# Attention with a gated feed-forward, one core: new cost entries, an extra VectorE block and new stretch rules in a kernel whose order is recorded by a planner

## The chip, the cores and the metric

The kernel runs on one core of one Trainium2 chip. A core has five engines that run side by side and wait for one another through semaphores: TensorE (PE, matrix products into the PSUM memory), VectorE (DVE), ScalarE (ACT), GpSimd (POOL, which works on the SBUF memory only in this kernel) and SyncE (SP, which issues most of the transfers). The metric is the device time of one execution in microseconds; less is better. The kernel before takes 671.5 us (median of 3 runs, 671.2 to 671.59).

## The reference

One sequence of 2048 positions and width 512. The input is normalised, and goes into an attention with 32 query heads of width 16 that share one key and one value head, and into a feed-forward with 1792 hidden channels. The attention is multiplied by a silu of the feed-forward, and the input is added.

```python
xn = _layernorm(x, axis=-1)                      # 2048 x 512
q = heads(xn @ wq)                               # 32 heads of 16
k = xn @ wk                                      # one head of 16
v = xn @ wv
scores = einsum("bhqd,bkd->bhqk", q, k) * 16 ** -0.5
p = softmax(scores)
s = merge(einsum("bhqk,bkd->bhqd", p, v)) @ wo
h = silu(xn @ w1) @ w2
return x + s * silu(h)
```

## The kernel before, in words

**Tiles and groups.** The queries are cut into 4 chunks of 512, the heads into 8 groups of 4, which gives 32 groups (chunk, heads). Each group meets 16 tiles of 128 keys, so there are 512 pairs of group and tile, and each has 4 blocks, one for each head: a block is the scores of 128 keys against 512 queries. There are 2048 blocks, and each has to be exponentiated. Scores are computed with the keys on the partitions, and a head has only 16 channels, so a score matmul uses 32 of the 128 rows of PE, and four of them, on four row tiles, can run side by side (L571).

**Two ways to exponentiate a block.** *ACT's way*: a run of two blocks is written into one of two PSUM tensors of 1024 columns (psA0 and psA1, in turn), and one activation with Exp turns both into weights in one of eleven slots of `pa_sb` (`exp_A`, L601). *DVE's way*: a block is written into one of three PSUM banks (`D`, `D1`, the two halves of psD, and `F`, psF, which the dense products use too). A tensor_scalar (`exp_D`, L639) adds a constant and clamps, and writes 16-bit integers whose bits, read as bf16, approximate the exponential. When the 4 blocks of a tile are there, POOL makes two more copies, shifted by constants, with int64 adds over four 16-bit numbers at a time (`shift`, L664). A tile of which DVE has only two blocks is shifted by DVE itself (L660). The three copies enter the sum with weights that are built into the values. Slots of DVE's tiles lie in `ph_sb`, and once the input has been used up a fourth lies in `x_sb`.

**PV.** Weights times values are accumulated in psO (`emit_PV`, L723), four column tiles side by side, one for each head of the group; an ACT block needs one such matmul, a DVE block three. When a group is complete, DVE transposes psO (L794), takes reciprocals (L802), multiplies (L811) and, every second group, transposes back (L821).

**Dense work.** Query projections, the two feed-forward products and the output projection go through bank F in jobs of column-tiled matmuls (`emit_job`, L363). Silu is built from a tanh on ACT (`emit_tanh`, L1039; 72 of them) and a multiply on DVE (L1071). `filler` issues matmuls on zeros where the planner finds PE too idle (L363 and, on whole tiles, L370).

**The start.** The first four of 16 row tiles are normalised with ACT's square root. For the three later groups of four tiles, DVE computes statistics (L379, L382), POOL the reciprocal deviation in two operations on 4 columns (`rstd_pow`, L386 an add, L388 a power), and DVE normalises (L400). Transposes, keys and values of these tiles come one after the other between runs of the first groups.

**What sets the order.** The function isn't written in the order in which it runs. `Sched` records operations: `op` appends one to its engine's queue, works out the semaphore waits from what it reads and writes, and estimates with fixed costs when it ends (`model`; 0.4 us on DVE and POOL where no cost is given). The main loop asks these estimates what to record next. Engines then run their queues strictly in the recorded order. In the loop, `score_run` records one ACT run and then calls `fill_D` (L1246), which places DVE blocks into banks that are free, first on the row tiles that the run leaves unused, so that they run beside it. Between two runs the loop fills PE with PV, dense jobs and fillers, up to the time by which ACT needs the next run (`needed`, `target` L1203 to L1213). `v_cand` and `advance_v` choose DVE's next operation.

**Rules per stretch.** A string PLAN names, for each 12 us of the recorder's time on ACT, one row of RULES: 12 numbers such as the slack when a bank counts as free (SLIP), the PE activity under which fillers are issued (KEEP), how long a DVE task waits in favour of blocks (AGE), how far dense work is brought forward (F_BEHIND), or how many tiles DVE may take ahead (LEAD).

Of the kernel before, what the change touches and what calls it, by code (L numbers as in the profile page):

```python
# [13 lines left out]
P = 128  # L14
# [182 lines left out]
def bass_recurrent_scan__grouped_kv_mqa__dense_activation_silu__prompt_kernel(  # L197
# [29 lines left out]
    NWARM = 15  # L227
    NWARM2 = 0
    NWARM3 = 2
    NFRONT = 12  # L230
    AGE2, AGE_ST, FIRST, FRONT_D, FRONT_K, SHORT, ST_EARLY, Q_ACT = 12.0, 1.5, 9.4, 1, 4, 0, 3, 1
    KEEP, ENDQ, ROUND, MAXJOB, AHEAD, Q_EARLY = 0.65, 12, 3.0, 2, 3, 0.18
    LEAD, LEAD_END, SLIP, AGE, AGE1, MARGIN = 3, 1, 0.2, 2.0, 1.2, 0.0
# [1 line left out]
    EV = "vava"  # L235
    PVWAIT, FKEEP = 0.2, 0.75
    NPAIR, LEAD_PAIR = 1, 1


    STRETCH = 12.0  # L240
    PLAN = (
        "AAAOFFAAJFNIAOEJAAGAKAALBACLAMFGKLFPNLFANFAEAAAQHAAODBA"
    )
    RULES = dict(
        A=(0.2, 3.0, 0.65, 10, 1.2, 2.0, 0, 12, 0.2, 3, 3, 0.0),
        B=(0.1, 3.0, 0.65, 10, 1.2, 2.0, 0, 12, 0.2, 3, 3, 0.0),
        C=(0.15, 3.0, 0.65, 10, 1.2, 2.0, 0, 12, 0.2, 3, 3, 0.0),
        D=(0.3, 3.0, 0.65, 10, 1.2, 2.0, 0, 12, 0.2, 3, 3, 0.0),
        E=(0.2, 3.0, 0.65, 11, 1.2, 2.0, 0, 12, 0.2, 3, 3, 0.0),
        F=(0.2, 3.0, 0.65, 10, 1.2, 2.0, 4, 12, 0.2, 3, 3, 0.0),  # L250
        G=(0.2, 3.0, 0.65, 10, 1.2, 2.0, 8, 12, 0.2, 3, 3, 0.0),
        H=(0.2, 3.0, 0.65, 10, 1.2, 2.0, 0, 24, 0.2, 3, 3, 0.0),
        I=(0.2, 3.0, 0.65, 7, 1.2, 2.0, 8, 12, 0.1, 3, 3, 0.0),
        J=(0.25, 3.0, 0.65, 8, 1.2, 2.0, 4, 12, 0.2, 3, 3, 0.0),
        K=(0.2, 3.0, 0.65, 7, 1.2, 2.0, -4, 12, 0.2, 3, 3, 0.04),
        L=(0.2, 3.0, 0.65, 10, 2.0, 3.0, 0, 12, 0.2, 3, 3, 0.04),
        M=(0.1, 3.0, 0.65, 10, 2.0, 3.0, 0, 12, 0.2, 3, 3, 0.0),
        N=(0.2, 3.0, 0.65, 10, 1.2, 1.0, 8, 12, 0.2, 3, 3, 0.04),
        O=(0.15, 3.0, 0.5, 10, 1.2, 2.0, 0, 12, 0.2, 2, 3, 0.0),
        P=(0.3, 3.0, 0.7, 10, 1.2, 2.0, 0, 6, 0.2, 3, 3, 0.0),  # L260
        Q=(0.25, 3.0, 0.65, 9, 1.2, 2.0, 0, 12, 0.2, 4, 3, 0.0),
    )
    NF, F_FROM, F_LEFT, F_LATE, DENSE_END, HOLD, F_BEHIND = 14, 0.05, 9, 3, 0.97, 10, 0

    with ExitStack() as es:
# [109 lines left out]
        def tiles(c):  # L375
            return range(4 * c, 4 * c + 4)
# [7 lines left out]
        def rstd_pow(c):  # L384
            sl = slice(4 * c, 4 * c + 4)
            op("gp", lambda e: e.tensor_scalar(rstd_sb[:, sl], mv_sb[:, sl, 1], LN_EPS, None, op0=ALU.add),  # L386
               reads=[("mv", t) for t in tiles(c)], writes=[("rstd", c)])
            op("gp", lambda e: e.tensor_tensor(rstd_sb[:, sl], rstd_sb[:, sl], mhalf_sb[:, :], ALU.pow),  # L388
               reads=[("rstd", c), "mhalf"], writes=[("rstd", c)])

        def rstd_sqrt(c):
            sl = slice(4 * c, 4 * c + 4)
# [193 lines left out]
        def held(key):  # L586
            return any(p["key"] == key for q in pend for p in q)
# [295 lines left out]
        def behind(by=0):  # L883
            return jst["slots"] + by < all_slots * (progress() - F0) / (F1 - F0)
# [67 lines left out]
        def free_banks(t):  # L952
            return [b for b in BANKS if hold[b] is None and K.ready("pe", [], [b]) <= t]

        def next_job(t):
            if progress() < F0:
                return None
            if sum(h == "job" for h in hold.values()) >= MAXJOB:
                return None
            return next((jb for jb in jobs[:AHEAD] if startable(jb, t)), None)  # L960
# [191 lines left out]
        def needed():  # L1152

            return K.act_end - 0.685 - MARGIN
# [47 lines left out]
        def target(t):  # L1202


            rel, need = max(release(), t), needed()
            if need <= rel:
                return rel
            used = [b for b in dst["fifo"]]
            idle = K.free["v"] + sum(0.6 for b in used)
            frees = [K.ready("pe", [], [b]) for b in BANKS if hold[b] is None]  # L1210
            f = min(frees) if frees else K.free["v"] + 0.65
            x = max(f, idle - 0.43)
            return min(max(rel, x), need) if x <= need + SLIP else need  # L1213

        def score_run(t):
            t = max(t, release())
            if ast["tile"] is None and not left[group_A()]:
                gi = group_A()
                h, kts, rows = halves[gi].pop(0)
                blocks = run_half(gi, h, kts, rows)  # L1220
                fill_D(t, other(rows))
                if tanh_ready(K.act_end - 0.33):
                    emit_tanh()
                exp_A(gi, blocks)
                return
            if ast["tile"] is None:
                gi = group_A()
                tile = ast["tile"] = (gi, left[gi].pop(0))
                if tile in shared:
                    rows = ast["rows"] = shared[tile]  # L1230
                todo = {i for o in dst["open"][:1] for i in o["todo"]}
                if tile not in shared:
                    rows = ast["rows"] = [0, 1] if len(todo & {2, 3}) >= len(todo & {0, 1}) else [2, 3]
                second = tile in shared
            else:
                tile, rows = ast["tile"], other(ast["rows"])
                second = True
            fill_A(tile, rows, state["n"] % 2)
            fill_D(t, other(rows))
            if tanh_ready(K.act_end - 0.33):  # L1240
                emit_tanh()
            exp_A(tile[0], [(i, tile[1], None, 512 * m) for m, i in enumerate(rows)])
            if second:
                ast["tile"] = None

        def fill_D(t, free):  # L1246

            banks = sorted(free_banks(t + SLIP), key=lambda b: (b == "F", K.ready("pe", [], [b])))
            keep = 0
            if "F" in banks and jobs and behind(F_BEHIND) and next_job(t):  # L1250
                keep = 1
            if front:
                keep = max(keep, len(banks) - 1 + sum(h == "blk" for h in hold.values()))
            for bank in banks[:max(0, len(banks) - keep)]:
                pick = [(o, i) for o in dst["open"] for i in o["todo"] if i in free]
                if not pick:
                    pick = [(o, o["todo"][0]) for o in dst["open"] if o["tile"][0] < group_A() or len(left[o["tile"][0]]) < F_LATE]
                if not pick and len(dst["open"]) < 2:
                    new, rows = next_D(t), [0, 1, 2, 3]
                    if new is not None:  # L1260
                        left[new[0]].remove(new[1])
                    else:
                        new, rows = next_half(t), [0, 1]
                    if new is not None:
                        plan_D(new[0], rows)
                        dst["idx"] += 1
                        slot_of[dst["idx"]] = free_slot(new[0])
                        dst["open"].append(dict(tile=new, todo=list(rows), rows=rows, idx=dst["idx"]))
                        pick = [(dst["open"][-1], i) for i in free if i in rows] or [(dst["open"][-1], rows[0])]
                if not pick:  # L1270
                    return
                o, i = pick[0]
                pos = len(o["rows"]) - len(o["todo"])
                o["todo"].remove(i)
                if not o["todo"]:
                    dst["open"].remove(o)
                burst([((o["tile"], i), bank_ap(bank))], [bank])
                dst["fifo"].append(dict(tile=o["tile"], i=i, bank=bank, idx=o["idx"], pos=pos, rows=o["rows"]))
                hold[bank] = "blk"
                if i not in free:  # L1280
                    return
                free.remove(i)
                if not free:
                    return
# [2 lines left out]
        K.free["a"] = max(K.free["a"], FIRST - 0.3)  # L1287
        now, gp_end = 0.0, False
        while state["g"] < NGRP or front or jobs or jst["open"] or tasks:
            (SLIP, ROUND, KEEP, HOLD, AGES["gn1"], AGE, F_BEHIND, ENDQ, PVWAIT, LEAD, AHEAD, MARGIN) = \  # L1290
                RULES[PLAN[min(int(K.act_end / STRETCH), len(PLAN) - 1)]]
            t = max(now, min(K.pe_next("col"), K.pe_next("full")))
            if t > 2000.0:
# [46 lines left out]
            if more and not blocked:  # L1340
                idle = slots - did
                if idle > 0 and K.activity(max(t, K.pe_last + K.pe_len) + 0.216 * idle) < (FKEEP if front else KEEP):
                    filler(idle)
                score_run(t)
                now = 0.0
            elif not did:
                if dst["open"]:
                    fill_D(t, [0, 1, 2, 3])
                now = t + 0.05
            else:  # L1350
                now = 0.0
# [96 lines left out]
```

## Time and profile before

| what | value |
|---|---|
| median of 3 runs | 671.5 us |
| the profiled execution | 673.14 us |
| its span from first to last instruction | 670.3 us |
| mean granted TensorE clock | 0.997 |
| first exponential (L601) starts, last one ends | 10.59 us, 663.14 us |
| tanh (L1039) | 72, mean 781 ns |
| single-block exponentials on DVE (L639, 128x512) | 684, mean 675 to 681 ns by group |
| double-block exponentials on DVE (L639, 128x1024) | 13, mean 1216 to 1224 ns |
| int64 adds on POOL (L664) | 354, mean 1048 ns |
| PV matmuls (L723) on 512 columns from ACT's, DVE's weights | 1330, 2130 |

The span leaves out what lies around the first and the last instruction, so it is compared with spans, and the median with medians. An engine's busy time counts overlapping instructions once. Matmuls are pipelined, so PE's 97% doesn't mean that PE has no room: four column matmuls start within 0.02 us of one another, and the next four 0.216 us later. In a group's line, the figures behind the bar are busy time, the mean duration of one, and the idle time of the engine just before, with what ended most of it.

### The profile page before, as it was taken

The numbers are of one execution on the slowest core, as the hardware profiler recorded it, in microseconds if no ns is written. First come the engines' busy times: TensorE is split into PE (matmuls) and PEld (weight loads), VectorE is DVE, ScalarE is ACT, GpSimd is POOL, SyncE is SP. The second block draws the span as 40 slices with busy tenths as digits, with TensorE's granted clock in tenths as the row PEclk, the third lists the DMA queues.
The fourth block names the chain that finished last, engine by engine and source line by source line (L and its number), as shares of the span: only waits on it lengthen the run. The fifth ranks groups of instructions, "written<-read, shape, count | busy, mean of one in ns | idle before, by whom it ended". The sixth has DMA issues, their size and how long they took to land.

```text
span 670.3 us, 18577 instructions
## 1 busy us (share of the span) xinstructions
PE 649.2 (97%) x8137; PEld 182.2 (27%) x8143; DVE 599.9 (90%) x1008; ACT 657.9 (98%) x755; POOL 375.0 (56%) x379
## 2 busy tenths in 40 slices
PE   8999999999999999999999999999999999999997
PEld 4422222222222222222222222222222222222222
DVE  7899889898888988999899889898899889888997
ACT  6999999999999999999999999999999999999997
POOL 3156546465565655555665566564565547656652
PEclk9999999899999999999999999999999999999999
DMA  6340000000000001000000000010000000000110
GB/s 174 139 147 1 2 2 1 2 1 2 2 1 2 1 18 34 17 2 2 1 2 2 1 2 2 1 34 17 18 2 1 2 2 1 2 2 1 34 33 31
DMA packets 12336, 12.48 MB, mean 19 GB/s; under 512 B 2528, under 2 KB 11744, under 8 KB 12256
## 3 DMA queue, kind: packets, MB, share of 16 engines
q1 hardware_dynamic: 11680, 10.78, 5.2%
q8 instruction: 63, 1.03, 0.6%
q10 hardware_dynamic: 576, 0.52, 0.2%
q14 instruction: 17, 0.14, 0.1%
HBM read 8.95 MB, written 2.10 MB: 16 GB/s over the span
## 4 chain that ended last, share of the span: by engine, by line
ACT 77%; PE 16%; DVE 6%; POOL 1%; DMA 0%; issue 0%; ACTq 0%
ACT pa_sb L601 72%; PE psA L571 5%; PE psO L723 5%; ACT t_sb L1039 5%; PE psF L363 4%; DVE ph_sb L639 1%; DVE stats_sb L379 1%; DVE xn_sb L400 1%; POOL rstd_sb L388 0%; PE psD L571 0%; DVE x_sb L639 0%; DMA x_sb<-in_A_x_dram 0%; PE psD L411 0%; DVE onb_sb L811 0%; PE psD L442 0%
## 5 line engine op out<-in xcount | busy, mean ns | idle before, releaser
L601 ACT ACTIVATE pa_sb<-psA 128x1024 bf16<-128x1024 f32 x669 | 636.5, 1202 | 3.2 <-PE psA L571 1.7
L664 POOL INT64_ADD ph_sb<-ph_sb x292 | 302.3, 1048 | 214.6 <-DVE ph_sb L639 214.4
L639 DVE TENSOR_SCALAR ph_sb<-psD 128x512 int16<-128x512 f32 x513 | 349.5, 692 | 40.1 <-PE psD L571 32.7
L723 PE MATMUL psO<-ph_sb,vaug_sb 128*32 128x512 bf16 x1758 | 218.3, 385 | 0.3
L723 PE MATMUL psO<-pa_sb,vaug_sb 128*32 128x512 bf16 (+1 forms) x1346 | 202.8, 383 | 0.6 <-DVE onb_sb L835 0.6
L571 PE MATMUL psA<-qT_sb,kTa_sb 32*128 32x512 bf16 x680 | 131.9, 384 | 4.5 <-ACT pa_sb L601 3.1
L571 PE MATMUL psA<-qT_sb,kTb_sb 32*128 32x512 bf16 x650 | 126.5, 386 | 7.0 <-ACT pa_sb L601 6.3
L571 PE MATMUL psD<-qT_sb,kTb_sb 32*128 32x512 bf16 x325 | 119.5, 385 | 1.0 <-DVE ph_sb L639 1.0
L571 PE MATMUL psD<-qT_sb,kTa_sb 32*128 32x512 bf16 x311 | 114.0, 384 | 0.0
L664 POOL INT64_ADD x_sb<-x_sb x62 | 64.3, 1049 | 44.9 <-DVE x_sb L639 44.9
L639 DVE TENSOR_SCALAR x_sb<-psD 128x512 int16<-128x512 f32 (+1 forms) x110 | 75.5, 691 | 11.7 <-PE psD L571 10.9
L571 PEld LDWEIGHTS psA<-qT_sb,kTa_sb 32*128 32x128 bf16 x680 | 32.0, 91 | 145.1 <-ACT pa_sb L601 131.2
L571 PEld LDWEIGHTS psA<-qT_sb,kTb_sb 32*128 32x128 bf16 x650 | 30.6, 91 | 144.7 <-ACT pa_sb L601 132.3
L363 PE MATMUL psF<-xnT_sb,w_sb 128*32 128x512 bf16 x896 | 69.6, 386 | 0.0
L363 PE MATMUL psF<-w_sb,u_sb 128*32 128x512 bf16 x896 | 69.2, 384 | 0.0
L723 PEld LDWEIGHTS psO<-ph_sb,vaug_sb 128*32 128x32 bf16 x1758 | 53.9, 95 | 51.2 <-issue 35.3
L723 PE MATMUL psO<-x_sb,vaug_sb 128*32 128x512 bf16 x372 | 65.9, 383 | 0.0
L723 PEld LDWEIGHTS psO<-pa_sb,vaug_sb 128*32 128x32 bf16 x1346 | 49.3, 95 | 43.5 <-issue 34.8
L1039 ACT ACTIVATE t_sb<-psF 128x512 bf16<-128x512 f32 x72 | 56.2, 781 | 0.0
L1071 DVE SCALAR_TENSOR_TENSOR u_sb<-t_sb,psF 128x512 bf16<-128x512 bf16 x56 | 38.2, 682 | 4.8 <-ACT t_sb L1039 3.6
L639 DVE TENSOR_SCALAR ph_sb<-psF 128x512 int16<-128x512 f32 x62 | 42.1, 680 | 0.0
L571 PEld LDWEIGHTS psD<-qT_sb,kTb_sb 32*128 32x128 bf16 x325 | 28.2, 91 | 2.4 <-DVE ph_sb L639 1.4
(125 smaller groups left out, 361.7 us busy)
## 6 DMA issues: line engine op xcount, KB each, us to landing
w_sb<-in_B_w_dram SPq DMA_DIRECT2D x2, 1792.0 KB, 8.9
x_sb<-in_A_x_dram SPq DMA_DIRECT2D x18, 128.0 KB, 2.3
out_dram<-ob_sb SPq DMA_DIRECT2D x14, 128.0 KB, 1.7
x_sb<-in_A_x_dram SPq DMA_DIRECT2D x3, 512.0 KB, 6.5
wop_sb<-in_A_wo_dram SPq DMA_DIRECT2D x1, 512.0 KB, 4.2
wq_sb<-in_A_wq_dram SPq DMA_DIRECT2D x1, 384.0 KB, 6.2
x_sb<-in_A_x_dram ACTq DMA_DIRECT2D x2, 128.0 KB, 2.8
kTb_sb<-kTa_sb SPq DMA_DIRECT2D x16, 16.0 KB, 1.8
```

What stands on the lines that cost most here:

```text
L363: r = e.matmul(bank[32 * i:32 * i + 32, :], lhsT=lhsT[:, 32 * i:32 * i + 32], rhs=rhs, start=start, stop=stop, tile_position=(0, 32 * i), ...
L379: op("v", lambda e: e.bn_stats(stats_sb[:, t, :], x_sb[:, t, :]), reads=[("x", t)], writes=[("st", t)], cost=0.687)
L400: op(eng, lambda e: e.tensor_scalar(xn_sb[:, t % 8, :], x_sb[:, t, :], mv_sb[:, t, 0:1], rstd_sb[:, t:t + 1], op0=ALU.subtract, op1=ALU.mult),
L571: return e.matmul(ap, lhsT=kT_sb[g % 2][32 * i:32 * i + 32, kt * P:(kt + 1) * P], rhs=qT_sb[32 * i:32 * i + 32, c % 2, g // 2, :], start=T ...
L601: d = op("a", lambda e: e.activation(pa_sb[:, sl, :], psA[k][:, :], ACT.Exp, scale=ESCALE), reads=["A%d" % k], writes=[("pa", sl)], cost=2 ...
L639: d = op("v", lambda e: e.tensor_scalar(ph_ap(0, sl, 512 * pos, 512 * pos + m), src, float(PH_ONE + PH_BIAS), 0.0, op0=ALU.add, op1=ALU.ma ...
L664: d = op("gp", lambda e, j=j: e.int64_add(ph_ap(j, sl, 0, 4 * NQ).bitcast(I64), ph_ap(0, sl, 0, 4 * NQ).bitcast(I64), PH_SHIFT[j] * 0x0001 ...
L723: r = e.matmul(psO[32 * i:32 * i + 32, cs], lhsT=vaug_sb[:, p["v"], p["kt"], :], rhs=p["ap"], start=s0, stop=s1, tile_position=(0, 32 * i) ...
L1039: op("a", lambda e: e.activation(t_sb[:, n % 2, :], bank_ap(b), ACT.Tanh, scale=0.5 if jb[0] == "h" else 0.25), reads=[b], writes=[("t", n ...
L1071: op("v", lambda e: e.scalar_tensor_tensor(out=dst, in0=t_sb[:, n % 2, :], scalar=1.0, in1=src, op0=ALU.add, op1=ALU.mult), reads=tk["read ...
```

## The change

The costs of the two POOL operations for the reciprocal deviation are given to the recorder (0.3 and 1.07 in place of the default 0.4 each). A new function `extra_fill`, called behind a run in stretches whose rule has XGAIN under 2, may place one more DVE block: it estimates when DVE will have nothing left, and takes the free bank that is ready soonest, at most XWAIT = 0.3 us from now, if DVE gains more than XGAIN plus the wait. The bank is passed to `fill_D`, which then leaves out its own choice of banks and the reservation of F. The lead of 0.43 in `target` becomes a number of the rule (AIM). NFRONT, the number of tiles before dense jobs may start, goes from 12 to 16. PLAN and RULES get new values, with two more columns (XGAIN and AIM); 14 of the 56 stretches of the new PLAN have an XGAIN under 2.

```diff
-    NFRONT = 12
+    NFRONT = 16
...
+    XHOLD, XTASK, XWAIT, XGAIN, XCOST, XOPEN, XBEH, AIM = 7, 0, 0.3, 9, 1.0, 0, 99, 0.43
...
     PLAN = (
-        "AAAOFFAAJFNIAOEJAAGAKAALBACLAMFGKLFPNLFANFAEAAAQHAAODBA"
+        "AAAJFHIPQRACARAAREKMLBPAHAOQDMDJAAJKHQGGQOFIRNIQFGGEMBBA"
     )
     RULES = dict(
-        A=(0.2, 3.0, 0.65, 10, 1.2, 2.0, 0, 12, 0.2, 3, 3, 0.0),
...
+        A=(0.2, 3.0, 0.65, 10, 1.2, 2.0, 0, 12, 0.2, 3, 3, 0.0, 9, 0.43),
...
+        R=(0.2, 3.0, 0.5, 10, 1.2, 1.5, 0, 12, 0.2, 3, 3, 0.0, 0.35, 0.43),
     )
...
             op("gp", lambda e: e.tensor_scalar(rstd_sb[:, sl], mv_sb[:, sl, 1], LN_EPS, None, op0=ALU.add),
-               reads=[("mv", t) for t in tiles(c)], writes=[("rstd", c)])
+               reads=[("mv", t) for t in tiles(c)], writes=[("rstd", c)], cost=0.3)
             op("gp", lambda e: e.tensor_tensor(rstd_sb[:, sl], rstd_sb[:, sl], mhalf_sb[:, :], ALU.pow),
-               reads=[("rstd", c), "mhalf"], writes=[("rstd", c)])
+               reads=[("rstd", c), "mhalf"], writes=[("rstd", c)], cost=1.07)
...
-            x = max(f, idle - 0.43)
+            x = max(f, idle - AIM)
...
-        def fill_D(t, free):
+        def extra_fill():
+
+            t = K.pe_last + K.pe_len
+            if sum(held(("pa", k)) for k in range(NPA)) >= XHOLD or group_A() >= NGRP or (XOPEN and jst["open"]) or (XBEH < 99 and behind(XBEH)):
+                return
+            advance_v(t + 0.05)
+            vfree = K.free["v"] + 0.62 * len(dst["fifo"]) + sum(tk["cost"] for tk in tasks if XTASK and all(n in tok for n in tk["need"]) and K.ready("v", tk["reads"], tk["writes"]) < t + 0.6)
+            ride = max(needed(), t + 0.2) + 0.43
+            best = None
+            for b in BANKS:
+                if hold[b] is None and (b != "F" or not jobs or not behind(F_BEHIND) or not next_job(t)):
+                    r = max(t, K.ready("pe", [], [b]))
+                    gain = max(vfree, ride) - max(vfree, r + 0.43)
+                    if r <= t + XWAIT and gain > XGAIN + XCOST * (r - t):
+                        if best is None or r < best[0]:
+                            best = (r, b)
+            if best is None:
+                return
+            fill_D(best[0], [0, 1, 2, 3], [best[1]])
+
+        def fill_D(t, free, only=None):
 
             banks = sorted(free_banks(t + SLIP), key=lambda b: (b == "F", K.ready("pe", [], [b])))
+            if only:
+                banks = only
             keep = 0
-            if "F" in banks and jobs and behind(F_BEHIND) and next_job(t):
+            if not only and "F" in banks and jobs and behind(F_BEHIND) and next_job(t):
                 keep = 1
...
                 score_run(t)
+                if XGAIN < 2:
+                    extra_fill()
```

More of the change, by code (lines that the diff above doesn't have):

```diff
@@ L237, in bass_recurrent_scan__grouped_kv_mqa__dense_activation_silu__prompt_kernel @@
     NPAIR, LEAD_PAIR = 1, 1
+    XHOLD, XTASK, XWAIT, XGAIN, XCOST, XOPEN, XBEH, AIM = 7, 0, 0.3, 9, 1.0, 0, 99, 0.43
     STRETCH = 12.0
     PLAN = (
-        "AAAOFFAAJFNIAOEJAAGAKAALBACLAMFGKLFPNLFANFAEAAAQHAAODBA"
+        "AAAJFHIPQRACARAAREKMLBPAHAOQDMDJAAJKHQGGQOFIRNIQFGGEMBBA"
     )
     RULES = dict(
-        A=(0.2, 3.0, 0.65, 10, 1.2, 2.0, 0, 12, 0.2, 3, 3, 0.0),
-        B=(0.1, 3.0, 0.65, 10, 1.2, 2.0, 0, 12, 0.2, 3, 3, 0.0),
-        C=(0.15, 3.0, 0.65, 10, 1.2, 2.0, 0, 12, 0.2, 3, 3, 0.0),
@@ L248, in bass_recurrent_scan__grouped_kv_mqa__dense_activation_silu__prompt_kernel @@
[L248 to L261, printed above, removed]
+        A=(0.2, 3.0, 0.65, 10, 1.2, 2.0, 0, 12, 0.2, 3, 3, 0.0, 9, 0.43),
+        B=(0.1, 3.0, 0.65, 10, 1.2, 2.0, 0, 12, 0.2, 3, 3, 0.0, 9, 0.43),
@@ new lines, in bass_recurrent_scan__grouped_kv_mqa__dense_activation_silu__prompt_kernel @@
+        C=(0.2, 3.0, 0.7, 10, 1.2, 2.0, 0, 12, 0.2, 3, 3, 0.0, 9, 0.43),
+        D=(0.2, 3.0, 0.65, 8, 1.2, 2.0, 0, 12, 0.2, 3, 3, 0.0, 9, 0.43),
+        E=(0.2, 3.0, 0.65, 11, 1.2, 2.0, 0, 12, 0.2, 3, 3, 0.0, 9, 0.43),
+        F=(0.2, 3.0, 0.65, 10, 1.2, 2.0, 4, 12, 0.2, 3, 3, 0.0, 9, 0.43),
+        G=(0.2, 3.0, 0.65, 10, 1.2, 2.0, 8, 12, 0.2, 3, 3, 0.0, 9, 0.43),
+        H=(0.2, 3.0, 0.65, 10, 1.2, 2.0, 0, 12, 0.2, 3, 3, 0.04, 9, 0.43),
+        I=(0.2, 3.0, 0.65, 10, 1.2, 2.0, 0, 12, 0.2, 3, 3, 0.0, 0.15, 0.43),
@@ new lines, in bass_recurrent_scan__grouped_kv_mqa__dense_activation_silu__prompt_kernel @@
+        J=(0.2, 3.0, 0.65, 10, 1.2, 2.0, 0, 12, 0.2, 3, 3, 0.0, 0.25, 0.43),
+        K=(0.2, 3.0, 0.65, 10, 1.2, 2.0, 0, 12, 0.2, 3, 3, 0.0, 0.35, 0.43),
+        L=(0.3, 2.5, 0.65, 10, 1.2, 2.0, -8, 12, 0.2, 3, 3, 0.0, 9, 0.43),
+        M=(0.2, 3.0, 0.65, 10, 1.2, 2.0, 0, 12, 0.2, 2, 2, 0.0, 9, 0.7),
+        N=(0.2, 2.75, 0.7, 10, 1.2, 2.0, 0, 12, 0.3, 3, 3, 0.0, 9, 0.43),
+        O=(0.2, 2.75, 0.65, 10, 1.2, 2.0, 0, 12, 0.2, 4, 3, 0.0, 0.05, 0.43),
+        P=(0.2, 3.5, 0.65, 10, 1.2, 2.0, 0, 12, 0.1, 3, 3, 0.04, 9, 0.43),
@@ L262, in bass_recurrent_scan__grouped_kv_mqa__dense_activation_silu__prompt_kernel @@
+        Q=(0.2, 3.0, 0.65, 10, 1.2, 2.0, 8, 12, 0.3, 3, 4, 0.0, 9, 0.43),
+        R=(0.2, 3.0, 0.5, 10, 1.2, 1.5, 0, 12, 0.2, 3, 3, 0.0, 0.35, 0.43),
     )
@@ L1289, in bass_recurrent_scan__grouped_kv_mqa__dense_activation_silu__prompt_kernel @@
         while state["g"] < NGRP or front or jobs or jst["open"] or tasks:
-            (SLIP, ROUND, KEEP, HOLD, AGES["gn1"], AGE, F_BEHIND, ENDQ, PVWAIT, LEAD, AHEAD, MARGIN) = \
+            (SLIP, ROUND, KEEP, HOLD, AGES["gn1"], AGE, F_BEHIND, ENDQ, PVWAIT, LEAD, AHEAD, MARGIN, XGAIN, AIM) = \
                 RULES[PLAN[min(int(K.act_end / STRETCH), len(PLAN) - 1)]]
```

## The prediction

> **What bounds the kernel now.** I read the page's busy shares, then the chain of work that ended last, then ScalarE's (ACT's) own timeline and idle time, and last the two places where ACT stood still.
>
> ```profile
> span 670.3 us, 18577 instructions
> PE 649.2 (97%) x8137; PEld 182.2 (27%) x8143; DVE 599.9 (90%) x1008; ACT 657.9 (98%) x755; POOL 375.0 (56%) x379
> ACT 77%; PE 16%; DVE 6%; POOL 1%; DMA 0%; issue 0%; ACTq 0%
> L601 ACT ACTIVATE pa_sb<-psA 128x1024 bf16<-128x1024 f32 x669 | 636.5, 1202 | 3.2 <-PE psA L571 1.7 <-PE psD L571 1.3
> L664 POOL INT64_ADD ph_sb<-ph_sb x292 | 302.3, 1048 | 214.6 <-DVE ph_sb L639 214.4
> ```
>
> ACT is the bound: 98% busy, 77% of the chain, and only 3.2 us idle before its 669 exponentials (L601), each over two 512-column blocks. The page's 1202 ns is a latency, since neighbours overlap; the pitch is in the chain in order of time:
>
> ```profile
> 433.07 19.25 ACT pa_sb L601 x21
> ```
>
> 19.25/21 = 0.917 us per exponential. From the first (10.59) to the end of the last (663.14) are 652.55 us: 669 x 0.917 = 613.5, 72 tanh at 0.48 (451.89 to 452.37) = 34.6, 3.2 idle, and 1.3 of small slips and the last one's latency. A block costs ACT 0.46 us; the same block given to VectorE (DVE, L639) costs ACT nothing. So the first question is how many exponentials are left; the second, whether ACT stays as full. These are its two largest stops after the start:
>
> ```profile
> 123.23 0.39 PE L571 MATMUL psA<-qT_sb,kTb_sb 32*128 32x512 bf16 x2 [0.53 <-ACT pa_sb L601]
> 125.00:126.00 1.00, 1.00 (x11) 0.10 (x3) 1.00 (x4) 1.00 (x3) 0.16 (x1) 0.50 0.00 0
> 126.00:127.00 1.00, 1.00 (x15) 0.34 (x16) 0.80 (x3) 1.00 (x2) 1.00 (x2) 0.50 0.00 0
> 128.28 2.86 ACT L601 ACTIVATE pa_sb<-psA 128x1024 bf16<-128x1024 f32 x3 [0.95 <-PE psD L571]
> ...
> 489.56 1.21 DVE L811 TENSOR_TENSOR onb_sb<-otr_sb,rcp_sb 128x256 bf16<-128x256 f32 x1
> 491.43 0.38 PE L571 MATMUL psD<-qT_sb,kTb_sb 32*128 32x512 bf16 x1 [0.47 <-DVE ph_sb L639]
> 492.72 3.77 ACT L601 ACTIVATE pa_sb<-psA 128x1024 bf16<-128x1024 f32 x4 [0.37 <-PE psD L571]
> ```
>
> The two window lines give busy time of PE, PEld, DVE, ACT and POOL, then the granted TensorE clock, DMA share and GB/s: the clock is at 0.50. After four runs with little work PE was slowed, and ACT lost 0.95. At 489 a normalising multiply took 1.21 us on DVE, where the fastest of its 31 took 0.41; the PSUM bank came free late, PE stood in order before it for 0.47, and ACT lost 0.37.
>
> **The change part by part.** Counts are from the order of both programs' instructions, durations from before.
>
> *Blocks moved.* ACT's exponentials fall from 669 to 664, tanh stay 72: 5 x 0.917 = -4.6 us on the path that sets the end. DVE gets the 10 blocks: single-block exponentials 684 to 686, double ones 13 to 17, and its two late shifts (L660) go: 2 x 0.681 + 4 x 1.216 - 2 x 0.806 = +4.6 us. Cover: DVE's waits for PE's scores, 43.6 + 1.8 us in L639's own answer. Without that cover DVE would be late by up to 4.6, at worst undoing the gain. POOL gets 360 adds for 354: 6 x 1.048 = 6.3 us, under its 260 us of waits for DVE (214.4 + 44.9).
>
> *PE's load.* A pass (four column matmuls side by side, or up to four row ones) is 0.216 us, a change of kind 0.1: in the chain a run's two scores take 0.32, eight PV matmuls 0.55, twelve 0.76. By the order, passes go from 2228.5 to 2232.5: +4 of PV (three shifted copies per DVE block against one from ACT), +21 for scores of DVE blocks that don't fit beside a run, -5 of runs, -16 of fillers and warmers. Intervals between runs with more work than ACT's pitch (a run plus three passes, 0.32 + 0.76 = 1.08 against 0.917; with a tanh in it, a run plus five) are 96 of 668 and become 94 of 663. PE's budget neither frees nor takes anything: 0, bounded by 4 x 0.216 = 0.9 on either side.
>
> *The new block behind a run.* 52 blocks come from it; 26 of them find an unused row tile and cost no pass, 26 cost one (they are in the count above). But they stand in PE's queue in front of PV and of the next run, waiting on DVE for a bank, and a bank of D or D1 is used again one run after its last use 48 times, against once before. So a late DVE reaches ACT sooner. The nearest row is the stop at 491: 0.37 a hit. Lower bound 0 (never late). The lateness comes from DVE operations with two SBUF inputs: 31 of L811 (mean 0.61, fastest 0.41) and 12 of L1050. If each extra makes two runs touchy, that's 48 of 663 runs, 7%, so 3 of 43 meet one; half of them late gives 1.5 x 0.37. I take +0.4; all 43 would be +15.9.
>
> *GpSimd's costs for the deviations.* The recorder believed 0.4 + 0.4 us; the trace has 0.24 + 1.04, and DVE waited 0.77, 0.30 and 0.90 for it:
>
> ```profile
> 26.80 1.04 POOL L388 TENSOR_TENSOR rstd_sb<-rstd_sb,mhalf_sb 128x4 f32<-128x4 f32 x1
> 27.88 1.38 DVE L400 TENSOR_SCALAR xn_sb<-x_sb,mv_sb,rstd_sb 128x512 bf16<-128x512 bf16 x4 [0.90 <-POOL rstd_sb L388]
> ```
>
> Now a BNStats (pitch 0.60), a K copy (0.32) and a V evacuation (0.32) stand in those gaps. What DVE gains is mostly spent on the blocks counted above; directly, ACT's idle before 34 us (0.17 + 0.17 + 0.19 + 0.42 = 0.95) can fall. The 0.42 hangs on the late DVE chain from 27.88; the rest on eight transposes in front of a run, which the new order has too. I take -0.3, between 0 and -0.95.
>
> *The clock.* Over four consecutive runs, passes x 0.216 over ACT's time (4 x 0.917, and 0.48 per tanh) is mostly about 0.7. The emptiest place before has 7 passes in four runs (0.41), and that is where the clock fell; the next, near 501 us, has 0.52 and kept 1.00. Now the emptiest two have 9 passes (0.53), fewer fillers (20 passes for 31) notwithstanding. I take the event as gone: -0.95. Bounds: 0 if one comes, +0.95 if two. The Trainium skill, "TensorE: Matmul & The Clock Gate", section "What's actually happening", says the clock halves after an idle window of about 3.4 us; here PE's gaps before the fall were 0.43 and 0.53 us, so the trace doesn't bear out a whole idle window, though the fall lasted about that long (0.64, 0.50, 0.50 and 0.66 in four windows of 1 us). By that rule neither program would lose anything to the clock, and the sum without this term would be 667.7.
>
> *The tail.* Behind the last run's scores PE went at once to the last group's half PV (661.68). Now three full PV passes stand between, since the last DVE tile is shifted on POOL and not on DVE: 3 x 0.216 = +0.65, and everything from the half transposes (L833) on follows; DVE's second half was right behind its first (663.19 + 0.45 = 663.64, next at 663.65), so nothing absorbs it. With some wait for POOL I take +0.7, between 0.6 and 1.2.
>
> *Other edits.* Four more tiles before the dense jobs (NFRONT) and the new rules are in the orders counted; SP's queue has the same 60 entries.
>
> Sum: -4.6 - 0.95 - 0.3 + 0.7 + 0.4 = -4.75, a span of 665.5. The profiled execution took 673.1 with its 670.3 span; the median of the runs is 671.5, 1.2 above the span. 665.5 + 1.2 = 666.7, or 671.5 - 4.75 = 666.8. I forecast 666.8.
>
> **The rivals.**
> 1. *The clock falls in the new thin places* (about 33 and 97 us): one or two events instead of none, 666.8 + 0.95 or + 1.9 = 667.8 to 668.7. For it: 16 passes less of filler and a share of 0.53. Against: 0.52 kept the clock.
> 2. *Slower: late DVE operations pass through PE to ACT.* Place: banks reused after one run; price 0.37; it eats the 4.75 from 13 more hits on. With 20 of the 43 hit, 666.8 + 20 x 0.37 = 674.2. For it: the chain at 489 to 492 is exactly this, and reuse after one run rises from 1 to 48. Against: only one such stop in 670 us before, though all 43 operations were there. The Trainium skill, "SBUF — State Buffer", section "SBUF: two separate sides", says that a DVE operation with two SBUF inputs and a GpSimd operation lock each other out for a whole instruction; L811's spread of 0.41 to 1.21 agrees with it.
> 3. *The change doesn't do what it says*: the blocks taken off ACT come back as waits of it, because PV, DVE or POOL feed the last tiles too late. ACT's idle then grows from 3.2 by the 4.6 saved: 671.4. Against it: every engine but ACT keeps idle time larger than what it gets.
>
> **How the numbers follow.** Forecast 0.72, rival 1 0.12, rival 2 0.08, rival 3 0.08. Forecast and rival 1 are faster: 0.84. A measurement here can't tell under 0.2% (1.3 us, 670.2 to 672.8) from no change: rival 3, 0.08. Slower: rival 2, 0.08. Low end: the whole front idle gone and no late hit, and half the 1.3 of slips: 666.8 - 0.65 - 0.4 - 0.65 = 665.1, say 665.0. High end: the clock rival's 668.7 and four more late hits, 670.0. The likeliest case's own range is 665.0 to 668.5.
>
> **What would show it.** ACT: 664 of L601 at 0.917, idle before them about 2.3 us (3.2 - 0.95 - 0.3 + 0.4). DVE's waits for POOL's deviation under 1 us in all, from 2.0. PEclk 1.00 in every slice past the start. L833's first transpose about 1.5 us behind the last run's scores, against 662.14 - 661.36 = 0.78. Wrong if ACT's idle before L601 is over 5 us, or waits of PE psD on DVE grow from some 3 us to over 10: then rival 2 is at work.

## The result, and the profile after

The changed kernel takes 665.08 us (median of 5 runs, 664.81 to 665.12) against 671.59 for the kernel before, measured beside it: a ratio of 0.990, 95% interval 0.9886 to 0.9914. It is faster by 6.5 us; 4.75 were forecast.

From the page of the changed kernel: span, busy shares, the chain that ended last, and the exponentials' group (out of in, count, then busy time and mean duration, then idle time before them and what ended it).

```profile
span 663.3 us, 18520 instructions
PE 651.5 (98%) x8114; PEld 183.8 (28%) x8114; DVE 599.3 (90%) x1012; ACT 652.5 (98%) x750; POOL 380.0 (57%) x385
PEclk9999999999999999999999999999999999999999
ACT 87%; PE 10%; DVE 1%; DMA 1%; SPq 0%; issue 0%; ACTq 0%
L604 ACT ACTIVATE pa_sb<-psA 128x1024 bf16<-128x1024 f32 x664 | 631.4, 1203 | 0.8 <-PE psA L574 0.6
```

ACT still bounds the kernel, and more than before: its share of the chain goes from 77% to 87%, PE's falls from 16% to 10%, and ACT's idle time before exponentials falls from 3.2 to 0.8 us. Of that 0.6 lies before the first one, as it did before. ACT's timeline shows it (start, duration, what, count; the first line and one near the end):

```profile
10.83 42.66 ACT L604 ACTIVATE pa_sb<-psA 128x1024 bf16<-128x1024 f32 x46 [0.59 <-PE psA L574]
...
629.63 25.95 ACT L604 ACTIVATE pa_sb<-psA 128x1024 bf16<-128x1024 f32 x28
```

46 exponentials follow one another from the first on, and ACT idles 0.2 us in all behind the first one; before there were four stops by 34 us. The account of the two profiled executions, first exponential to end of the last, with 0.917 us for an exponential and 0.48 for a tanh:

| | before | after | difference |
|---|---|---|---|
| first exponential starts | 10.59 | 10.83 | +0.24 |
| exponentials and tanh at their pitch | 613.5 + 34.6 | 608.9 + 34.6 | -4.6 |
| idle of ACT behind the first exponential | 2.6 | 0.2 | -2.4 |
| small slips (what is left of 652.55 and 644.75) | 1.85 | 1.05 | -0.8 |
| from the last exponential's end to the span's end | 7.16 | 7.72 | +0.56 |
| span | 670.3 | 663.3 | -7.0 |

So -4.6 of the -7.0 are the five exponentials, -3.2 more come from an ACT that hardly stops any longer, and the later start and the longer tail give 0.8 back. The 2.4 of idle time are 0.95 at the start, 0.95 at the fall of the clock near 128 us and 0.5 of other stops, of which the one at 492 us has 0.37. The later start is scatter between executions: with the changed kernel's order the first exponential started at 10.54 in experiment 8. The spans differ by 7.0 and the medians by 6.5, because the profiled execution of before had a fall of the clock that most of its executions don't have (see the third experiment); without its 0.95 the span of before is 669.35, and the difference 6.1.

### The profile page after: what moved, and what is told of

The parts are those of the page before. It is cut to its first block, busy times and chain, and to the rows that moved or that the text cites. A ratio compares the mean times of both kernels' runs of the same rounds, so it can differ in the third digit from the quotient of the medians.

```text
span 663.3 us, 18520 instructions
## 1 busy us (share of the span) xinstructions
PE 651.5 (98%) x8114; PEld 183.8 (28%) x8114; DVE 599.3 (90%) x1012; ACT 652.5 (98%) x750; POOL 380.0 (57%) x385
## 4 chain that ended last, share of the span: by engine, by line
ACT 87%; PE 10%; DVE 1%; DMA 1%; SPq 0%; issue 0%; ACTq 0%
ACT pa_sb L604 82%; ACT t_sb L1042 5%; PE psA L574 3%; PE psO L726 3%; PE psF L366 2%; PE psD L414 0%; PE psD L445 0%; DMA x_sb<-in_A_x_dram 0%; DVE stats_sb L382 0%; DMA kTb_sb<-kTa_sb 0%; SPq L463 0%; PE psA L620 0%; PE psD L574 0%; DVE xn_sb L403 0%; ACT ob_sb L1396 0%
## 5 line engine op out<-in xcount | busy, mean ns | idle before, releaser
L667 POOL INT64_ADD ph_sb<-ph_sb x284 | 293.0, 1044 | 199.8 <-DVE ph_sb L642 199.6
L642 DVE TENSOR_SCALAR ph_sb<-psD 128x512 int16<-128x512 f32 (+1 forms) x505 | 343.0, 695 | 34.0 <-PE psD L574 28.4
L726 PE MATMUL psO<-ph_sb,vaug_sb 128*32 128x512 bf16 x1704 | 212.6, 383 | 0.0
L726 PE MATMUL psO<-pa_sb,vaug_sb 128*32 128x512 bf16 (+1 forms) x1336 | 196.5, 382 | 0.1
L574 PE MATMUL psD<-qT_sb,kTb_sb 32*128 32x512 bf16 x339 | 125.3, 384 | 0.7 <-DMA kTb_sb<-kTa_sb 0.2
L667 POOL INT64_ADD x_sb<-x_sb x76 | 78.7, 1047 | 50.1 <-DVE x_sb L642 50.1
L642 DVE TENSOR_SCALAR x_sb<-psD 128x512 int16<-128x512 f32 x139 | 95.5, 696 | 11.3 <-PE psD L574 10.6
L726 PE MATMUL psO<-x_sb,vaug_sb 128*32 128x512 bf16 x456 | 81.4, 383 | 0.0
L642 DVE TENSOR_SCALAR ph_sb<-psF 128x512 int16<-128x512 f32 x50 | 34.0, 681 | 0.0
```

The costliest lines, as they stand in the source:

```text
L574: return e.matmul(ap, lhsT=kT_sb[g % 2][32 * i:32 * i + 32, kt * P:(kt + 1) * P], rhs=qT_sb[32 * i:32 * i + 32, c % 2, g // 2, :], start=T ...
L642: d = op("v", lambda e: e.tensor_scalar(ph_ap(0, sl, 512 * pos, 512 * pos + m), src, float(PH_ONE + PH_BIAS), 0.0, op0=ALU.add, op1=ALU.ma ...
L667: d = op("gp", lambda e, j=j: e.int64_add(ph_ap(j, sl, 0, 4 * NQ).bitcast(I64), ph_ap(0, sl, 0, 4 * NQ).bitcast(I64), PH_SHIFT[j] * 0x0001 ...
L726: r = e.matmul(psO[32 * i:32 * i + 32, cs], lhsT=vaug_sb[:, p["v"], p["kt"], :], rhs=p["ap"], start=s0, stop=s1, tile_position=(0, 32 * i) ...
```

## The experiments

The recorder's order hangs on every estimate, so an edit of a feature alone changes the whole order behind it. Two kinds of experiment were made: kernels that are recorded anew with one part on or off, and kernels that keep one order on every engine and change what some instructions do.

**1. GpSimd's costs alone.** In the kernel before:

```diff
-               reads=[("mv", t) for t in tiles(c)], writes=[("rstd", c)])
+               reads=[("mv", t) for t in tiles(c)], writes=[("rstd", c)], cost=0.3)
...
-               reads=[("rstd", c), "mhalf"], writes=[("rstd", c)])
+               reads=[("rstd", c), "mhalf"], writes=[("rstd", c)], cost=1.07)
```

> The kernel before with one edit: the recorder is given 0.3 and 1.07 us for GpSimd's two operations of the deviations; PLAN, RULES and NFRONT stay as they were. By the order ACT now has 684 exponentials instead of 669. Theory A (the gain is in the number of exponentials, and that number hangs on PLAN fitting the recorder's estimates): 15 x 0.917 = +13.8 us, less up to 1 of front idle and 0.95 if the clock holds: 683 to 686 us. Theory B (knowing GpSimd's time is by itself a gain, since DVE's 2.0 us of waits for it go): faster than before by 1 to 2 us, 669.5 to 670.5.

Measured: 683.89 us, ratio 1.0175 (1.0162 to 1.0188). Theory A holds for the total: 684 exponentials. But theory B's mechanism is there too, only small against that. In windows from 10 to 34 us (busy time of PE, PEld, DVE, ACT and POOL, then clock, DMA share, GB/s) the kernel before has

```profile
10.00:34.00 24.00, 22.33 (x256) 10.24 (x255) 21.01 (x55) 22.46 (x24) 4.28 (x8) 1.00 0.37 121
```

and with GpSimd's costs alone

```profile
10.00:34.00 24.00, 23.49 (x279) 10.60 (x278) 22.19 (x58) 23.29 (x27) 6.06 (x9) 1.00 0.39 126
```

and in its table of waits (total, times, longest)

```profile
DVE xn_sb L400 <- POOL rstd_sb L388: 0.2, 1, 0.2
```

DVE's 2.0 us of waits for the deviations are down to 0.2, and ACT works 0.83 us more in the stretch. In the changed kernel the same stretch has 23.29 for ACT as well. Experiment 9 is the reverse test: the changed kernel's source with the two costs at their default and without the extra block. All four stops are back there:

```profile
14.84 2.85 ACT L604 ACTIVATE pa_sb<-psA 128x1024 bf16<-128x1024 f32 x3 [0.23 <-PE psA L574]
17.87 4.69 ACT L604 ACTIVATE pa_sb<-psA 128x1024 bf16<-128x1024 f32 x5 [0.17 <-PE psA L574]
22.74 8.44 ACT L604 ACTIVATE pa_sb<-psA 128x1024 bf16<-128x1024 f32 x9 [0.19 <-PE psA L574]
31.60 13.98 ACT L604 ACTIVATE pa_sb<-psA 128x1024 bf16<-128x1024 f32 x15 [0.42 <-PE psA L574]
```

Experiment 10, with the costs and still without the extra block, has none of them. The start's gain is therefore the cost entries', and it is 0.83 (0.95 in idle time).

**2. Without the extra block.** In the changed kernel:

```diff
-                if XGAIN < 2:
+                if False:
                     extra_fill()
```

> The changed kernel without the call of extra_fill; all numbers as in the change. By the order 679 exponentials instead of 664. Theory A: 15 x 0.917 = +13.8 us, and ACT about as full as in the changed kernel: 678 to 680 us. Theory B (the extra block only crowds PE, and a bank reused after one run makes ACT wait): without it ACT waits less, and the time stays under 672.

Measured: 679.33 us, ratio 1.0116 (1.0101 to 1.0131), with 679 exponentials. Theory A. Experiment 1 adds a part to numbers that were chosen without it, experiment 2 takes one away from numbers that were chosen with it, and each costs 15 exponentials. That says how well PLAN fits its recorder, and not yet what a part is worth; experiments 9 to 11 ask that.

**3. The thin place.** In the kernel before, with the same order:

```diff
-                burst([((o["tile"], i), bank_ap(bank))], [bank])
+                burst([((o["tile"], i), bank_ap(bank))], [bank], 3 if state["n"] in (112, 114) else 1)
...
```

where the third argument says how often the scores are computed.

> The kernel before, same order on every engine, but the scores of two DVE blocks behind runs 112 and 114 are computed three times (four more passes in the emptiest place). Theory A (the clock fell because PE had 7 passes in four runs): PEclk 1.00 throughout, ACT's stop of 0.95 goes, 670.6 us, ratio 0.9986. Rival (the fall comes by chance or from something else): PEclk 0.50 near 125 us as before, 671.5.

Measured: 671.33 us beside 672.0, ratio 0.9992 (0.9983 to 1.0001). The profile has no fall of the clock, and ACT no stop at this place:

```profile
122.00:126.00 4.00, 3.81 (x43) 1.13 (x46) 4.00 (x9) 4.00 (x6) 2.05 (x2) 1.00 0.00 0
```

That shows less than it seems to, since most executions of before have no fall either. The span and the mean granted clock of each run are known. Of 65 runs of before beside these experiments 13 have a clock of 0.997 or less and spans of 670.1 to 671.7, like the profiled execution (0.997, 670.3); the 38 runs of up to 671.6 us have 0.998 or more and spans of 669.1 to 669.8. The other 14 are longer at a clock of 0.998 or more. This kernel's 11 runs all have 0.998 or more; if each had a fall with before's share of 13 in 65, none in 11 would still come about one time in 12. So the four passes may prevent the fall, but that isn't shown, and the interval of the times holds no change. What the runs do show is that the median which the forecast started from, 671.5, lies among the executions without a fall, and against that the changed kernel has no 0.95 to gain.

**4. Without the fillers.** In the changed kernel, same order, `filler` issues 64 columns instead of its passes, on psO and, where it warms a free bank, there:

```diff
-                    for _ in range(n):
-                        r = columns(e, psO, zero_sb[:, 0:P], zero_sb[:, :], False, False)
-                    return r
+                    return columns(e, psO[:, 0:64], zero_sb[:, 0:P], zero_sb[:, 0:64], False, False)
...
```

> The changed kernel, same order, but each filler is cut to 64 columns (20 passes of column fillers and 7 of whole-tile ones nearly gone). Without them the emptiest four runs (near 33 us) have a share of 0.41, as where the clock fell before. Theory A: the clock falls there once, ACT loses about 0.95 and waits: 666.0 us. Rival (the fillers are not needed): 665.1, PEclk 1.00.

Measured: 665.04 to 678.95 in 12 runs, median 676.1; the spread is the finding, so no ratio is given. One run is as fast as with fillers, most lose up to 14 us, far more than the 0.95 of theory A. In the profiled one (span 674.2) the clock falls at 14 us and stays down until about 37; it falls once more between 44 and 52 us. Three of the windows:

```profile
16.00:20.00 4.00, 4.00 (x22) 1.51 (x20) 2.07 (x5) 2.74 (x3) 0.00 (x0) 0.50 0.80 234
24.00:28.00 4.00, 4.00 (x32) 1.91 (x32) 1.81 (x4) 3.22 (x4) 0.00 (x0) 0.50 0.00 0
32.00:36.00 4.00, 4.00 (x36) 1.46 (x33) 3.47 (x8) 2.82 (x3) 0.00 (x0) 0.50 0.16 39
```

PE is busy in all of each window, as the profile counts it, and still gets half the clock, and ACT works 2.3 to 3.2 us of 4 between 16 and 36 us. Some 27 passes, under 6 us of PE's time, keep up to 14.

**5 and 6. A late DVE, put in by hand.** In both kernels, same order, the 31 reciprocals (L805 and L802) are issued four times each, and the recorder's clock is set back so that it doesn't know:

```diff
...
+            was, end = K.free["v"], K.at[d]
+            for _ in range(3):
+                d = op("v", lambda e: e.reciprocal(rcp_sb[:, sl, :], o3[:, :, DH]), reads=tk["reads"], writes=tk["writes"], cost=tk["cost"])
+                K.at[d] = end
+            K.free["v"] = was
```

> The changed kernel, same order on every engine, but each of 31 groups' reciprocals is computed four times: DVE is 3 x 0.16 = 0.48 us late at 31 places, without the recorder knowing. Rival 2 of the prediction (a bank reused after one run hands a late DVE to ACT): far more than in the kernel before, up to 31 x 0.37 = 11.5 us, so 670 to 677. Theory A (PE does stop more often for a bank, but two psA tensors and DVE's waits for scores take it up): ACT's idle grows by under 3 us, 665 to 668.

> The same three extra reciprocals per group in the kernel before, same order. Rival 2: banks are reused after two runs, so under 2 us more, 671.5 to 673.5, clearly less than the changed kernel loses. Theory A: about the same loss in both, 0 to 3 us.

Measured: the changed kernel 682.96 us, 17.9 more than its 665.08 in the first comparison; the kernel before 688.9, 17.7 more than the 671.23 beside it. Some of these runs have falls of the clock too; the one of each with the highest clock has a span of 679.8 and 686.2, 17 more than 663.0 to 663.3 and 669.4. The added instructions took more than their chain pitch: 93 in a group of their own, 253 ns each.

```profile
L808 DVE RECIPROCAL rcp_sb<-otr_sb 128x16 f32<-128x16 f32 x93 | 23.6, 253 | 3.2
```

The losses were expected far too small in both kernels, 0 to 12 us; only "about the same loss in both" came true. That speaks against rival 2: the loss is the same where banks are reused after one run (48 times) and where they aren't (once). It doesn't rule the rival out, since the lateness was put at the ends of the 31 groups, and not where the extra blocks are. Of some 27 us of added DVE time (23.6 and 3.2 of idle before them), 17 to 18 reach the end in either order. DVE is the second bound: lateness that the order doesn't know of is only partly taken up.

**7 and 8. No late multiplies.** In both kernels, same order, the 31 normalising multiplies (L811, L814) are replaced by a memset of their output, so both leave the normalisation of the attention out:

```diff
-            op("v", lambda e: e.tensor_tensor(d3, o3, rcp_sb[:, sl, :].unsqueeze(2).to_broadcast([P, NQ // 32, DH]), ALU.mult),
+            op("v", lambda e: e.memset(d3, 0.0),
```

> The kernel before, same order, but the 31 normalising multiplies of DVE (two SBUF inputs, mean 609 ns, fastest 406) are memsets of the same output, so the normalisation of the attention rows is left out: DVE is never late there. Theory C (part of the gain was that the new order meets fewer late multiplies): the stop of 0.37 at 492 us goes and so do small slips, 670.0 to 671.0. Rival (late multiplies cost nothing beyond the one stop): 671.1.

> The same replacement in the changed kernel, same order; the normalisation of the attention rows is left out. Its multiplies averaged 544 ns. Theory C: little is left to gain, 664.8 to 665.1. Rival 2 of the prediction (late multiplies pass to ACT through banks that are reused after one run): more than in the kernel before, 663 to 664.

Measured: before 670.21 against 671.35, ratio 0.9981 (0.9972 to 0.999); the changed kernel 664.63, against 665.08 in the first comparison, between its two expectations. So 1.1 us hang on these multiplies before and 0.45 or less after (the kernel before was 0.24 faster here than in the first comparison), a difference of 0.7 to 0.9. That fits theory C. It is an upper bound for the lateness alone, since a memset takes 0.165 us and even an undelayed multiply 0.41. The durations fit too. Laid against POOL's timeline, 16 of the 31 multiplies before start while an add of POOL runs and take 0.79 us on average, the other 15 take 0.41; after, 14 start under an add and take 0.70, and 17 take 0.41. At 489 us before, the second of two adds and the multiply:

```profile
489.46 1.04 POOL L664 INT64_ADD ph_sb<-ph_sb  x1
489.56 1.21 DVE L811 TENSOR_TENSOR onb_sb<-otr_sb,rcp_sb 128x256 bf16<-128x256 f32 x1
```

The multiply starts 0.10 us into the add and ends at 490.77, 0.28 after it. All 30 multiplies that start under an add end 0.27 to 0.28 us after that one add, so what each takes hangs on how far the add has come. The new order has no multiply over 0.79 us. That it has fewer long ones isn't planned by the recorder, which gives each of them 0.43. Experiments 5 and 6 are not mirrored here: of 27 us that DVE gets on top without the order's knowing, 17 to 18 reach the end, but some 14 us taken off DVE (31 times 0.61 - 0.165) bring the kernel before only 1.1.

**9, 10 and 11. A plan for each recorder.** The changed kernel's source with both new parts off, with GpSimd's costs only, and with both; for each, PLAN was chosen anew from the change's rules by searches of the same size:

```diff
-        "AAAJFHIPQRACARAAREKMLBPAHAOQDMDJAAJKHQGGQOFIRNIQFGGEMBBA"
+        "AAMFGGAMHGAHHFCACAGGAHBHEBFHEAAGBEBACBGHAGHEGHAHGHLAFLAA"
...
+        "AAAFFHGGAHFGBAHLGGCFGGAAGEMGGEHGAHGAHHMFGGGGFCAEBFDMHHAA"
...
+        "AAAFGIIIJKIJJAECIAEIGAHMAHGGDHIFCAAACFGHFGAHGAAAFEAAGAAA"
```

in this order: both off, GpSimd's costs, both.

> The changed kernel with both new parts switched off (no extra_fill, GpSimd's two operations at the default 0.4 us), and PLAN chosen anew for this recorder by a beam search of 8 plans, stretch by stretch, among the rules of the change; the best of three such searches. By the order 672 exponentials. Theory A (the time is the number of exponentials at 0.917 us plus what the recorder has wrong): against the changed kernel's 665.1 it is 8 x 0.917 = +7.3, and +0.9 for the start's wrong costs: 672.5 to 674.

> The same with GpSimd's real costs and no extra_fill, PLAN from a search of the same size. By the order 670 exponentials. Theory A: 6 x 0.917 = +5.5 on 665.1: 670 to 671.5. If knowing GpSimd's time is worth something, this is clearly under the kernel with both parts off (by 1.8 for exponentials and up to 0.9 for the start).

> The same with both new parts, PLAN from a search of the same size (42 extra blocks). By the order 670 exponentials. Theory A: 670 to 671.5, as without the extra block; then the extra block by itself brings nothing that a search of this size finds, and what is left of the change's gain (6 exponentials) is the longer choice of its numbers. Theory B (the extra block is what lifts the limit): clearly under the kernel without it.

Measured beside 671.45 for the kernel before: both off 673.66 (ratio 1.0033, 1.002 to 1.0046), GpSimd's costs 670.3 (0.9977, 0.9968 to 0.9987), both 671.7 (1.0006, 0.9997 to 1.0015), the last a little above its 670 to 671.5. The plan that knows GpSimd's time is 3.4 us faster: 1.8 are two exponentials, 1.0 the stops at the start, and 0.5 the rest. The stops are the costs' doing (experiment 1). For the two exponentials that isn't shown, since each recorder has one plan here, and how far two searches of this size differ by chance wasn't measured. The extra block brings nothing in searches of this size: with it and without it 670 exponentials, and 1.4 us more. A difference that fits is in the two kernels' multiplies (minimum, median, maximum in ns), first with GpSimd's costs alone, then with both:

```profile
L814 DVE TENSOR_TENSOR onb_sb<-otr_sb,rcp_sb x31: 406/415/1211, 42.2 to 647.4; 128x256 bf16<-128x256 f32 x31
```

```profile
L814 DVE TENSOR_TENSOR onb_sb<-otr_sb,rcp_sb x31: 406/605/1209, 42.2 to 648.7; 128x256 bf16<-128x256 f32 x31
```

and in ACT's timeline of the second

```profile
632.01 30.36 ACT L604 ACTIVATE pa_sb<-psA 128x1024 bf16<-128x1024 f32 x33 [0.37 <-PE psD L574]
```

20 of the second's multiplies start under an add, for 13 of the first's, and ACT stops 0.37 us once, the same price as in the kernel before; its idle time before exponentials is 1.9 for 1.1. That this stop comes from a multiply isn't shown: the last long one ended 3.7 us before ACT went on. The changed kernel's own numbers give 664 exponentials with both parts. What as long a choice of numbers would have reached without the extra block wasn't found out, so the five exponentials are the whole change's, and not shown to be the extra block's.

## Why the prediction was right or wrong, step by step

**The bound and the exponentials: right.** ACT sets the time, 664 exponentials at 0.917 us, -4.6.

**GpSimd's costs, -0.3 forecast: -0.83 to -0.95.** The forecast left three of the four stops at the start in place, because eight transposes still stand in front of a run. They do (from 14.26 us in the changed kernel, from 13.55 in the one before), but in the kernel before PE came to them late, after waiting 0.33 for DVE. With DVE on time, all four stops went; that the second psA tensor then covers the transposes is our reading.

**The extra block, +0.4 forecast: the wrong sign.** This is the step that failed most. Its own working gives 1.5 x 0.37 = 0.56, of which 0.4 was taken, and it used the 48 reuses of a bank for the touchy runs, where two for each of 52 blocks would be 104. PE does wait for DVE at a bank more often, as the forecast said; the listings for DVE's exponentials (L639 before, L642 after) say who waited for them (us, times):

```profile
  PEld psD L571: 1.9, 5
  PE psD L571: 1.0, 3
```

```profile
  PEld psD L574: 8.2, 28
...
  PE psD L574: 0.6, 2
```

2.9 us became 8.8, and yet ACT stops less. The waits are short, 0.3 us on average, and a run is due only 0.917 us after the last one; ACT would notice a DVE that is late by more than that slack. Where +0.4 was counted, the stops outside the start and the clock went from 0.7 to 0.2, and small slips down by 0.8. The new order met fewer long multiplies, which by experiments 7 and 8 is worth 0.7 to 0.9; how much of the stops and the slips that is isn't separated.

**The clock, -0.95: right for the profiled execution, nothing for the median.** The fall isn't in the changed kernel's profile. But the forecast took it off 671.5, which is the time of executions without a fall, and it added the 1.2 between that median and the span of another execution, one with a fall. Time and span of one execution differ by 1.8 in most runs. That the thin place is the cause isn't shown (experiment 3).

**The tail, +0.7 forecast: +0.56.** The first half transpose starts 655.29 - 653.87 = 1.42 us behind the last run's scores, for 0.78 before; 1.5 was forecast.

**PE's load at 0, DVE's and POOL's additions hidden: right.** DVE's busy time is 599.3 for 599.9, POOL's 380.0 for 375.0. DVE's 4.6 more don't show in its busy time, in part because the multiplies take 2.0 less in sum.

**A slip of the forecast's own account:** the 3.2 us of idle time include 0.59 before the first exponential, which it counted behind it; small slips were 1.85 and not 1.3, and no term was given to their change.

**The rivals.** 1: no fall came at 33 or 97 us. 2: DVE's lateness does reach ACT, but nothing in the runs shows that the reuse of banks has a part in it, and in the change it didn't happen. 3: no, ACT's idle time fell.

In sum the mechanism of the largest term was right and the gain came out too small. Without the clock, from which the median had nothing to gain, 3.8 us were forecast. The spans without a fall differ by 6.1, 2.3 more: the start 0.6, the other stops and slips 1.7 (0.4 lost was forecast, 1.3 were gained), and the tail with the later start take back 0.1. That the total was only 1.75 off was luck in part, since a clock term that wasn't there made up for a part of the stops and slips.

## What to carry to other kernels

Where one engine bounds a kernel whose order is fixed in advance, count its instructions in both orders first; then ask how late its feeders are, because an engine at 90% that hands on its lateness is a second bound even when it has 1% of the chain, as DVE has here after the change. A planner's gain lies as much in estimates that hold on the chip as in new moves: two wrong estimates for GpSimd's operations cost 0.95 us of stops at the start, where a new kind of block brought nothing in searches of equal size. And a part that is tested with numbers chosen for another planner tells how well they fit, not what the part is worth.

## What the runs showed of the hardware that wasn't expected

The granted clock of TensorE stayed at 0.50 from 16 to 36 us although PE was busy in the whole of these windows (experiment 4), after less filler in the first 14 us; with fillers the changed kernel's clock is at 9 tenths or more in every slice of the page. A DVE multiply with two SBUF inputs that starts under an int64 add of GpSimd waits for that one add, and ends 0.27 to 0.28 us after it: 0.46 to 1.21 us in all, for 0.41 alone, by how far the add had come. An add that follows at once doesn't keep it out any longer; that add takes 1.20 us in place of 1.04. And the same three added reciprocals per group cost two quite different orders the same 17 to 18 us.
